# Block sums of the values: one batch stays on TensorE, the other goes to VectorE

## The chip, the cores and the metric

One core of one Trainium2 chip runs the whole program. The metric is the device time of one execution in microseconds; a kernel's time is the median over its runs. The profile is of one further execution, whose span is measured from its first to its last instruction.

## What is computed

An attention layer over 2 batches, 8 heads, 768 positions and 64 dimensions a head, followed by two feed-forward layers. Each query sees the keys at a distance below 16, and one summary for each block of 32 keys (24 blocks). A summary's key is the maximum of the block's keys, its value the mean of the block's values. Only that mean is touched here:

```
v_sum = v.reshape(B, H, nb, block, D).mean(axis=3)
scores_s = scale * einsum('bhsd,bhnd->bhsn', q, k_sum) + log(block)
a = softmax(concatenate([scores_l_masked, scores_s], -1))
attn = a @ concatenate([v, v_sum], axis=2)
x = (attn_x @ w_a) * (attn_x @ w_b) @ w_out
h = x @ w_in;  out = maximum(0.01 * h, h) @ w_out2
```

## The kernel before

The 1,536 tokens are three chunks of 512. Attention is cut into 12 pairs, four to a chunk; a pair is two groups of 256 queries of two heads each. For a pair the kernel transposes the queries (`q_prep`, L508), multiplies them with the keys window by window (`scores`, L526), takes the row minimum of the negated scores with the mask added on VectorE (L539) and the exponential on ScalarE (L543), divides by the sum (`normal`, L551 to L553, VectorE), transposes the result (`p_transpose`, L561, copied out by L563) and multiplies with the values (`pv`, L573, written out by L583 and L584). Block maxima of keys are taken in `k_prep` (L480 to L497). In what follows "(6,0)" is the first group of pair 6; pairs 6 and later hold batch 1. At most two scores tiles (`pm`) and two transposed ones (`pt`) are alive.

`load_vb` brings a batch's values as six tiles of 128 half blocks, 16 rows of 64 dimensions each. `v_sums` (twice for a batch) multiplies them with the matrix `place`, which adds neighbouring half blocks and divides by 32, and a VectorE reduction (L453) adds the eight row slots left in the bank. `v_place` (L463) moves the rows of the eight heads to partitions 0 to 23, L470 copies them out, and GpSimd (L189) spreads them into the value windows that `pv` multiplies. Both batches use the same six tiles; afterwards these buffers become `x` tiles.

The feed-forward weights arrive as fp64 and are made fp32 pairs on the chip by `convert`, seven steps a piece: `low` (L338 VectorE, L342 ScalarE), `clamp` (L346), `shift` (L351), `join` (L357), `add` (L363), `high` (L368, ScalarE), `rest_of` (L371). The steps wait in a list, `bg`. `tick(n)` takes n of them from its head; `weights(key)` takes as many as it needs until the piece that is to be multiplied is done. Every step is tied behind the latest L539 issued so far:

```
with tc.issue_after(pace["after"].ins) ...:
    bg.pop(0)()
```

The first pieces are, in order, a0, b0, a1, b1, a2, b2, a3, b3, o0 to o3. Products of the first chunk with a0 to b1 run inside attention; a2, b2, a3, b3 follow as `first_product` (L591, 12 matmuls each), and after each half of such a product `interleave` runs a share of the remaining attention operations of pairs 4 to 7 (they are sorted by an order number) and then `tick(4)`. There are eight such places before the output products of the first chunk (with o0 to o3). The program is written in this order; the scheduler then lets each engine take, at any moment, the earliest written instruction whose inputs it believes ready.

Of the kernel before, what the change touches and what calls it, by code (L numbers as in the profile page):

```python
# [11 lines left out]
F32 = mybir.dt.float32  # L12
# [4 lines left out]
ALU = mybir.AluOpType  # L17
AX = mybir.AxisListType
# [3 lines left out]
def kernel(  # L22
# [12 lines left out]
    nc = tc.nc  # L35
    B, H, S, D = q.shape
    P = 128
    BLK = 32
    WIN = 16
    NB = S // BLK  # L40
# [41 lines left out]
    sm_p = att.enter_context(tc.tile_pool(name="sm", bufs=4))  # L82
# [9 lines left out]
    def at_bank():  # L92
        cnt["at"] += 1
        return bank(at_banks[cnt["at"] % len(at_banks)])
# [26 lines left out]
    NV = 2 * H * NB // P  # L121
    vb_tiles = [xp.tile([P, BLK // 2, D], F32, tag="x", name=f"vb{j}") for j in range(NV)]
    vs_t = {}
    bg = []

    pace = {"micro": 0.0, "bg": 3, "after": None}
    q_t, k_t, vb_t, vw_of = {}, {}, {}, {}
# [68 lines left out]
    LOAD, SIDE, PRODUCT = range(3)  # L196
# [3 lines left out]
    def attention_ops():  # L200

        ops = []
        seen = set()
        for i, p in enumerate(sum(pairs, [])):

            def add(at, kind, f, *args):
                ops.append((PER * i + at, kind, lambda: f(*args), i))

            for m, (b, hp) in enumerate(dict.fromkeys(x[:2] for x in p)):
                if (b, hp) not in seen:  # L210
                    seen.add((b, hp))
                    add(-18, LOAD, load_k, b, hp)
                    for j in range(2):
                        add(2 * m + j + -12, PRODUCT, k_prep, b, hp, j)
                    if hp == 0:
                        add(-5, LOAD, load_vb, b)
                        for j in range(2):
                            add(1 + j, PRODUCT, v_sums, b, j)
                        add(7, PRODUCT, v_place, b)
            add(-14, LOAD, load_q, i, p)  # L220
            add(-6, PRODUCT, q_prep, i, p)
            for j in range(2):
                add(4 * j, PRODUCT, scores, i, p, j)
                add(4 * j + 3, SIDE, normal, i, j)
                add(4 * j + 8, PRODUCT, p_transpose, i, j)
            add(1, LOAD, load_vw, i, p)
            add(9, SIDE, put_sums, i, p)
            add(PV, PRODUCT, pv, i, p)
        ops.sort(key=lambda o: o[:2])
        return ops  # L230
# [19 lines left out]
    for c in range(2):  # L250
        for o, c0, c1 in ((0, 0, W), (W, SC, P)):
# [3 lines left out]
                out=loc, in_=loc, compare_op=ALU.is_ge, fill=BIG,  # L255
# [3 lines left out]
                out=loc, in_=loc, compare_op=ALU.is_ge, fill=BIG,  # L259
# [10 lines left out]
    V0 = 32  # L270
    place = const.tile([P, P], F32, tag="place", name="place")
    nc.gpsimd.memset(place, 1.0 / BLK)
    for base, pattern, mult in ((2 * V0, [[-2, P]], 1), (1 - 2 * V0, [[2, P]], -1)):

        nc.gpsimd.affine_select(
            out=place, in_=place, compare_op=ALU.is_ge, fill=0.0,
# [150 lines left out]
    def v_sums(b, j):  # L427
# [26 lines left out]
            out=vb_t[b][:, j], in_=ps.rearrange("p (j d) -> p d j", d=D), op=ALU.add, axis=AX.X  # L454
        )

    def v_place(b):

        v0 = vb_t.pop(b)
        ps = at_bank()  # L460
        for h in range(H):
            j, r = divmod(h, HQ)
            nc.tensor.matmul(  # L463
                out=ps[0:NB, h * D : (h + 1) * D],
                lhsT=ident[:, r * V0 : r * V0 + NB],
                rhs=v0[:, j],
                start=True, stop=True,
            )
        vs = sm_p.tile([NB, H, D], F32, tag="vs", name="vs", bufs=2)
        nc.scalar.copy(out=vs, in_=ps[0:NB].rearrange("p (h d) -> p h d", h=H))  # L470
        vs_t[b] = vs
# [165 lines left out]
    n_first = len(pairs[0])  # L637
    end = PER * (n_first - 1) + PV
    ops = attention_ops()
    for kt in range(NP):  # L640
        ops.append((PER * kt + PV + 5, PRODUCT, lambda kt=kt: early(kt), 0))
# [30 lines left out]
    def first_product(key, src, c):  # L672

        w = weights(key)
        ps = product_bank(key[0])
        for kt in range(KT):
            kt_mm(ps, w, src[c, kt], kt)
            if kt == KT // 2 - 1:
                interleave()
        return ps  # L680
# [114 lines left out]
    for f, c in slices2:  # L795
        ps = first_product(("i", f), ysp, c)
        h = g_p.tile([P, T], F32, tag="g", name="h")
        nc.scalar.copy(out=h, in_=ps)  # L798
        nc.vector.scalar_tensor_tensor(  # L799
            out=h, in0=h, scalar=0.01, in1=ps, op0=ALU.mult, op1=ALU.max  # L800
# [41 lines left out]
```

## Time and profile before

| | |
|---|---|
| time, median of 3 runs | 662.0 us (661.85 to 664.17) |
| the profiled execution | 662.39 us, of which the span is 660.7 us |
| PE (TensorE matmul) busy | 643.6 us, 97% of the span |
| DVE (VectorE) busy | 413.1 us, 63% |
| ACT (ScalarE) busy | 268.6 us, 41% |
| POOL (GpSimd) busy | 21.2 us, 3% |

The shares are means over the whole span; attention, on which the change works, ends for the first two chunks within the first 120 us, and is read in stretches of its own. A matmul of fp32 numbers appears as two records in this kernel's attention part.

### The profile page before, as it was taken

The numbers are of one execution on the slowest core, as the hardware profiler recorded it, in microseconds if no ns is written. First come the engines' busy times: TensorE is split into PE (matmuls) and PEld (weight loads), VectorE is DVE, ScalarE is ACT, GpSimd is POOL, SyncE is SP. The second block draws the span as 40 slices with busy tenths as digits, with TensorE's granted clock in tenths as the row PEclk, the third lists the DMA queues.
The fourth block names the chain that finished last, engine by engine and source line by source line (L and its number), as shares of the span: only waits on it lengthen the run. The fifth ranks groups of instructions, "written<-read, shape, count | busy, mean of one in ns | idle before, by whom it ended". The sixth has DMA issues, their size and how long they took to land.

```text
span 660.7 us, 9453 instructions
## 1 busy us (share of the span) xinstructions
PE 643.6 (97%) x3520; PEld 520.1 (79%) x3520; DVE 413.1 (63%) x960; ACT 268.6 (41%) x607; POOL 21.2 (3%) x39
## 2 busy tenths in 40 slices
PE   6798999999999999999999999999999999999997
PEld 4576767777888888888888888888888888888886
DVE  4978889955999972699633869732279532422323
ACT  4667767653445421344221535322255322222221
POOL 3111011000000000000000000000000000000000
PEclk9999999999999999999999999999999999999999
DMA  9977526411344430233200132400014000100101
GB/s 235 245 180 182 136 71 162 134 26 64 108 143 132 154 101 0 64 126 112 82 0 1 63 97 70 154 1 0 1 46 146 0 1 0 65 1 0 64 0 65
DMA packets 72591, 53.45 MB, mean 81 GB/s; under 512 B 46176, under 2 KB 66656, under 8 KB 72544
## 3 DMA queue, kind: packets, MB, share of 16 engines
q1 hardware_dynamic: 72544, 52.84, 27.7%
q8 instruction: 28, 0.46, 0.3%
q14 instruction: 19, 0.16, 0.1%
HBM read 49.68 MB, written 3.15 MB: 80 GB/s over the span
## 4 chain that ended last, share of the span: by engine, by line
PE 91%; DVE 4%; SPq 2%; DMA 1%; ACT 1%; issue 1%; ACTq 0%
PE ps_t L591 38%; PE ps_c L591 19%; PE ps_a L591 14%; PE ps_b L591 14%; PE ps_t L526 3%; PE ps_t L573 2%; PE ps_t L561 2%; PE ps_t L445 1%; SPq L175 1%; DMA wst<-in_moe_w_a_dram 1%; DMA wst<-in_moe_w_b_dram 1%; PE ps_t L508 1%; DVE pm L553 1%; SPq L132 0%; DVE pm L539 0%
## 5 line engine op out<-in xcount | busy, mean ns | idle before, releaser
L591 PE MATMUL ps_t<-x,wsp 128*128 128x512 f32 x336 | 78.6, 389 | 0.0
L591 PE MATMUL ps_c<-wsp,gs 128*128 128x512 f32 x288 | 75.8, 389 | 0.0
L591 PE MATMUL ps_t<-wsp,gs 128*128 128x512 f32 x288 | 74.7, 389 | 0.0
L591 PEld LDWEIGHTS ps_t<-x,wsp 128*128 128x128 f32 x336 | 63.1, 188 | 13.1
L591 PE MATMUL ps_t<-ys,wsp 128*128 128x512 f32 x288 | 71.9, 389 | 0.0
L591 PE MATMUL ps_a<-x,wsp 128*128 128x512 f32 x252 | 66.3, 399 | 1.4 <-DVE x L584 1.0
L342 ACT ACTIVATE wc<-wst 128x512 f32<-128x512 f32 x68 | 45.7, 675 | 53.7 <-DMA wst<-in_moe_w_out_dram 16.4
L591 PE MATMUL ps_b<-x,wsp 128*128 128x512 f32 x252 | 65.9, 395 | 0.0
L591 PEld LDWEIGHTS ps_t<-ys,wsp 128*128 128x128 f32 x288 | 54.1, 188 | 11.2
L591 PEld LDWEIGHTS ps_c<-wsp,gs 128*128 128x128 f32 x288 | 54.0, 188 | 11.2
L591 PEld LDWEIGHTS ps_t<-wsp,gs 128*128 128x128 f32 x288 | 54.0, 188 | 11.2
L591 PE MATMUL ps_c<-gs,wsp 128*128 128x512 f32 x240 | 60.3, 391 | 0.0
L591 PEld LDWEIGHTS ps_a<-x,wsp 128*128 128x128 f32 x252 | 46.4, 188 | 12.0 <-DVE x L584 1.5
L591 PEld LDWEIGHTS ps_b<-x,wsp 128*128 128x128 f32 x252 | 46.9, 188 | 9.8 <-issue 0.3
L799 DVE SCALAR_TENSOR_TENSOR h<-h,ps_t 128x512 f32<-128x512 f32 x24 | 16.5, 688 | 60.8 <-ACT h L798 60.8
L371 DVE TENSOR_TENSOR wsp<-wc,wsp 128x512 fp32r<-128x512 f32 x68 | 47.4, 700 | 9.1 <-ACT wsp L368 8.9
L591 PEld LDWEIGHTS ps_c<-gs,wsp 128*128 128x128 f32 x240 | 44.7, 188 | 9.3
L368 ACT CAST wsp<-wc 128x512 fp32r<-128x512 f32 x68 | 42.1, 622 | 20.5 <-DVE wc L363 13.9
L591 PE MATMUL ps_t<-gs,wsp 128*128 128x512 f32 x192 | 47.7, 390 | 0.0
L612 DVE TENSOR_TENSOR gs<-h,gs 128x512 fp32r<-128x512 f32 x48 | 33.1, 692 | 22.8 <-ACT gs L611 22.7
L363 DVE CUSTOM_DVE_ANT_0 wc<-wc,wr 128x1024 uint16<-128x1024 uint16 x68 | 46.9, 689 | 0.5
L357 DVE SCALAR_TENSOR_TENSOR wc<-wst,wc 128x512 int32<-128x512 int32 x68 | 46.5, 688 | 0.2
(89 smaller groups left out, 840.3 us busy)
## 6 DMA issues: line engine op xcount, KB each, us to landing
wst<-in_moe_w_out_dram SPq DMA_DIRECT2D x28, 512.0 KB, 3.3
wst<-in_moe_w_in_dram SPq DMA_DIRECT2D x16, 512.0 KB, 3.8
wst<-in_moe_w_a_dram SPq DMA_DIRECT2D x12, 512.0 KB, 3.8
wst<-in_moe_w_b_dram SPq DMA_DIRECT2D x12, 512.0 KB, 3.6
k<-in_k_dram SPq DMA_DIRECT2D x16, 192.0 KB, 4.5
vb<-in_v_dram SPq DMA_DIRECT2D x6, 512.0 KB, 5.2
out_dram<-acc SPq DMA_DIRECT2D x12, 256.0 KB, 2.1
q<-in_q_dram SPq DMA_DIRECT2D x16, 128.0 KB, 3.5
```

Of the source, the lines that this page charges most:

```text
L175: nc.sync.dma_start(out=t[p0 : p0 + o1 - o0, c, w0:w1, :], in_=src)
L342: nc.scalar.activation(out=t["c"].bitcast(F32), in_=hi_w.bitcast(F32), func=AF.Abs)
L357: nc.vector.scalar_tensor_tensor(out=t["c"], in0=hi_w, scalar=-0x40000000, in1=t["c"], op0=ALU.bitwise_and, op1=ALU.bitwise_or,)
L363: nc.vector.tensor_tensor(out=t["c"], in0=t["c"], in1=t["r"], op=ALU.add)
L368: nc.scalar.copy(out=t["w"][:, 0], in_=t["c"].bitcast(F32))
L371: nc.vector.tensor_tensor(out=t["w"][:, 1], in0=t["c"].bitcast(F32), in1=t["w"][:, 0].bitcast(F32), op=ALU.subtract,)
L526: nc.tensor.matmul(out=ps[h, w, :], lhsT=qt[h, w * W : (w + 1) * W], rhs=kts[h, (g * G + w) * SC : (g * G + w) * SC + P], start=True, stop ...
L561: nc.tensor.transpose(ps[:, w, :], pm[:, w, :], ident)
L573: nc.tensor.matmul(out=ps[c * D : (c + 1) * D, j * GT + w * W : j * GT + (w + 1) * W], lhsT=vw[:, c, j * G + w, :], rhs=pt[:, w, c * W : ( ...
L591: nc.tensor.matmul(out=ps, lhsT=w(a), rhs=x(b), start=first and j == 0, stop=last and j == 2)
L612: nc.vector.tensor_tensor(out=t[:, 1], in0=src, in1=t[:, 0].bitcast(F32), op=ALU.subtract)
L799: nc.vector.scalar_tensor_tensor(out=h, in0=h, scalar=0.01, in1=ps, op0=ALU.mult, op1=ALU.max)
```

## The change

For batch 0 nothing is changed. For batch 1 the two calls of `v_sums` go. In their place, earlier in the order (order number 44 in place of 49 and 50), `v_sums_later` puts twelve VectorE reductions at the head of `bg`: two for each of the six tiles, each adding the 16 rows of a half block for 32 of the 64 dimensions, straight from SBUF. They are taken by `tick`, four at a place, ahead of what is left of the conversions. `v_place` first takes whatever of the twelve is still in the list; for batch 1 it multiplies the tiles of half block sums with `place`, which now adds the halves, divides and moves in one: ten matmuls (five for each four heads) where there were eight.

```diff
+                        if b == 0:
+                            for j in range(2):
+                                add(1 + j, PRODUCT, v_sums, b, j)
+                        else:
+                            add(-4, SIDE, v_sums_later, b)
...
+    def v_sums_later(b):
+        vb_t[b] = v0 = sm_p.tile([P, NV, D], F32, tag="v1", name="v1", bufs=1)
+        bg[0:0] = [
+            lambda i=i, d=d: nc.vector.tensor_reduce(
+                out=v0[:, i, d : d + D // 2],
+                in_=vb_tiles[i][:, :, d : d + D // 2].rearrange("p j d -> p d j"),
+                op=ALU.add, axis=AX.X,
+            )
+            for i in range(NV)
+            for d in (0, D // 2)
+        ]
+        vb_done.append(bg[2 * NV - 1])
...
     def v_place(b):
+        while vb_done and vb_done[-1] in bg:
+            bg.pop(0)()
         v0 = vb_t.pop(b)
         ps = at_bank()
-        for h in range(H):
+        for h in range(H) if b else ():
+            r0, r1 = 2 * h * NB, 2 * (h + 1) * NB
+            tiles = range(r0 // P, (r1 - 1) // P + 1)
+            for i in tiles:
+                c0 = V0 + (r0 - i * P) // 2
+                nc.tensor.matmul(
+                    out=ps[0:NB, h * D : (h + 1) * D],
+                    lhsT=place[:, c0 : c0 + NB],
+                    rhs=v0[:, i],
+                    start=i == tiles[0], stop=i == tiles[-1],
+                )
+        for h in range(H) if not b else ():
```

## Rows read from the trace of the kernel before

**Rows 1.** The page, busy time of each engine, and PE's busy tenths in 40 slices.
```profile
PE 643.6 (97%) x3520; PEld 520.1 (79%) x3520; DVE 413.1 (63%) x960; ACT 268.6 (41%) x607; POOL 21.2 (3%) x39
PE   6798999999999999999999999999999999999997
```

**Rows 2.** Busy time by stretch; columns: stretch, length, engines, granted clock, DMA share, GB/s.
```profile
60.00:64.00 4.00, 2.93 (x14) 2.15 (x13) 4.00 (x9) 3.17 (x12) 0.00 (x0) 1.00 0.78 206
...
73.00:81.00 8.00, 8.00 (x70) 6.19 (x65) 7.36 (x19) 6.01 (x22) 0.00 (x0) 1.00 0.41 116
81.00:87.20 6.20, 6.20 (x49) 1.90 (x46) 2.63 (x12) 2.13 (x9) 0.00 (x0) 1.00 0.08 19
87.20:92.00 4.80, 4.80 (x75) 4.06 (x76) 4.76 (x17) 3.63 (x12) 0.00 (x0) 1.00 0.62 154
```

**Rows 3.** The chain that ended last, 77 to 92 us; columns: start, us, what.
```profile
77.14 0.46 PE ps_a L591 x2
...
77.82 2.32 PE ps_a L591 x10
80.14 1.02 PE ps_t L526 x16
81.16 1.85 PE ps_t L445 x16
...
83.60 3.60 PE ps_t L445 x24
87.20 0.59 PE ps_t L508 x4
87.78 0.44 PE ps_t L561 x4
...
89.24 0.56 PE ps_t L463 x8
89.80 1.08 PE ps_t L573 x32
...
91.44 0.66 PE ps_b L591 x2
```

**Rows 4.** The timeline of DVE, 72 to 92 us; idle before in brackets.
```profile
72.95 0.69 DVE L363 CUSTOM_DVE_ANT_0 wc<-wc,wr 128x1024 uint16<-128x1024 uint16 x1
73.55 0.68 DVE L553 TENSOR_TENSOR pm<-pm,sm 128x512 f32<-128x512 f32 x1
...
74.75 0.42 DVE L338 TENSOR_SCALAR wr<-wst 128x512 int32<-128x512 uint32 x1
...
75.35 0.69 DVE L371 TENSOR_TENSOR wsp<-wc,wsp 128x512 fp32r<-128x512 f32 x1
...
77.18 0.69 DVE L623 TENSOR_TENSOR g<-ps_b,g 128x512 f32<-128x512 f32 x1 [0.24 <-PE ps_b L591]
...
80.46 0.31 DVE L497 COPY kts<-ks 128x288 f32<-128x288 f32 x1
83.64 0.29 DVE L539 CUSTOM_DVE_ANT_0 pm<-ps_t,negm_first 128x128 f32<-128x128 f32 x1 [2.87 <-PE ps_t L561]
...
85.47 0.69 DVE L453 TENSOR_REDUCE v<-ps_t 128x64 f32<-128x512 f32 x1 [0.56 <-PE ps_t L445]
86.08 0.42 DVE L346 TENSOR_SCALAR wc<-wc 128x512 f32<-128x512 f32 x1
...
90.74 0.42 DVE L338 TENSOR_SCALAR wr<-wst 128x512 int32<-128x512 uint32 x1
91.08 0.68 DVE L371 TENSOR_TENSOR wsp<-wc,wsp 128x512 fp32r<-128x512 f32 x1
```

**Rows 5.** PE by stretch, earlier in attention; columns: stretch, length, PE, granted clock, DMA.
```profile
30.00:32.00 2.00, 1.17 (x7) 0.87 1.18 312
32.00:34.00 2.00, 2.00 (x11) 0.50 1.13 216
34.00:36.00 2.00, 2.00 (x31) 0.78 0.89 262
```

More of the change, by code (lines that the diff above doesn't have):

```diff
@@ L123 @@
     vs_t = {}
-    bg = []
+    bg, vb_done = [], []
     pace = {"micro": 0.0, "bg": 3, "after": None}
@@ L216, in attention_ops @@
                         add(-5, LOAD, load_vb, b)
-                        for j in range(2):
-                            add(1 + j, PRODUCT, v_sums, b, j)
+                        if b == 0:
[3 more added lines that the diff above has]
+                            add(-4, SIDE, v_sums_later, b)
                         add(7, PRODUCT, v_place, b)
```

## The prediction, made before the changed kernel was built or run

> **What bounds the kernel now.** I read the page first: TensorE is busy for 643.6 of 660.7 us, and after the first five of the 40 slices it never falls below nine tenths [rows 1]. VectorE's 63% is a mean that hides what matters here, so I went to the stretches. From 60 to 64 us PE is busy for only 2.93 of 4 us while DVE has no idle moment; from 64 us on PE is full, and from 73 to 81 us DVE works 7.36 of 8 us beside it [rows 2]. So the last part of attention is close to balanced: PE sets the time, DVE runs at its heels. Between 81 and 87.2 us the picture turns, PE full, DVE busy for 2.63 us only [rows 2]. That is batch 1's `v_sums`: on the chain of waits its matmuls (L445) hold 1.85 and 3.60 us [rows 3], and on DVE's timeline the pause shows as 2.87 us ahead of L539, which waits for a transpose (L561) that PE issued between the two calls [rows 4]. The last thing to see is how late the weights are made. Counting L371, the seventh ends a3 at 75.35 us and the eighth b3 at 91.08 [rows 4]; PE begins with a3 at 77.14 and with b3 at 91.44 [rows 3]. The conversions are made just before they are used, on the engine that now gets more to do.
>
> **What goes.** Both calls of `v_sums` of batch 1: 1.85 + 3.60 = 5.45 us of PE [rows 3]. The 40 records take far less than the sum of their durations because four column groups run beside each other, so I take their place on the chain and not their durations. PE has no pause around them, so all of it is on the path. On DVE two L453 go, 0.61 us each (85.47 to 86.08) [rows 4], 1.22 us together.
>
> **What comes on PE.** `v_place` of batch 1 has ten matmuls for eight. The eight are 16 records, two groups like that at 89.24 us with 0.56 us for 8 records [rows 3], 0.07 us a record. Two matmuls are four records, 0.28 us. If PE never waited, the change would be worth 5.45 - 0.28 = 5.17 us. The six loads of values are the same ones, and their tiles come free after the reductions as before after the matmuls: nothing is priced there.
>
> **What comes on DVE.** Twelve reductions of 512 numbers a partition. No reduction from SBUF stands in the trace; L453, also over 512 strided numbers but from PSUM, takes 0.61 us. The cheapest DVE row of that size from SBUF is L338, 0.34 us (90.74 to 91.08) [rows 4]; the dearest reading is the full 0.69 us of L453 with nothing overlapped. I take 0.61, the row that is the same operation: 7.32 us, between 4.1 and 8.3. The Trainium skill (VectorE: DVE Perf Modes, The perf-mode tier table) gives tensor_reduce a single rate wherever its data lies, while single-source operations on SBUF run at up to twice that; by it the low end falls away, and the sum stays at 7.32 us. L453 bears it out for PSUM; for SBUF no row here does. The Trainium skill's rules for kernel authors on the same page go further and advise to restructure such reductions on a hot path, which is the opposite of this change; what that would do here is the forecast below.
>
> **Where the twelve land.** They are taken four at a time at the second, third and fourth of the eight places in the first chunk's products. The first eight are tied behind (5,1)'s L539, which ends at about 72.95 us, the last four behind (6,1)'s. The list's tail moves with them: a3's `add`, `high` and `rest_of`, which before came in the second place, are now taken after the twelve, by `weights` ahead of a3's product, so behind (6,1)'s L539; b3 follows behind (7,0)'s and (7,1)'s. So DVE does not merely get 7.3 us more, it gets them ahead of a3.
>
> DVE until a3: before, its work from 72.95 us ends at 80.77 (80.46 + 0.31) with one pause of 0.24 [rows 4]. I take out that pause, a3's L363 (0.60) and L371 (0.60, the spacing of its size) and b3's L338 (0.34), and put in eight reductions (4.88): 80.77 - 0.24 - 1.54 + 4.88 = 83.87 us. The four L539 of a group take 0.85 us: from 83.64 to 84.91 (85.47 less its pause of 0.56) lie four of them and one L346 of 0.42 [rows 4]. With (6,0) and (6,1) it is 85.57; four reductions, 2.44, make 88.01; (6,0)'s L553 0.60 and a3's L363 0.60, 89.21; the cast on ScalarE, put at 0.60 by the same size, 89.81. Only then can PE begin with a3.
>
> PE until a3: without a3's first two matmuls it is free at 77.82 - 0.46 = 77.36 us [rows 3]. What it can do until then is attention: three score groups (6,0), (6,1), (7,0), 3 x 1.02; three transposes at 0.44, 1.32; two query transposes at 0.59, 1.18; `pv` of pair 5, 1.08; `v_place`, 1.12 + 0.28 [rows 3]. That is 8.04 us in a stretch of 12.45 us. **The cover is gone: PE idles for about 4.4 us**, because a3's product, which filled this stretch before, now lies behind it. No other filler exists: b3 comes later still, the output products need o0, and the second chunk's products need pairs 6 and 7. After 89.8 us a3 and b3, each 2.78 us (0.46 + 2.32), cover the rest of pairs 6 and 7, and once pair 7 is through, PE has the second chunk's products with weights that are ready. I count no further idle time.
>
> What is late next: the pieces o0 to o3 move back by twelve steps too. They are wanted by the first chunk's output products, and PE can put second-chunk products before those. I price this at nothing; without that cover it costs up to the steps of one piece, three of 0.34 and three of 0.60 us, 2.8 us.
>
> **The sum.** 662.39 us of the profiled execution - 5.17 + 4.4 = 661.6. The median of the three runs is 0.4 us below the profiled one, so I forecast 661.2 us, for a measurement that tells about 0.5%, 3.3 us, from no change. With reductions at 0.34 us a3 is ready 12 x 0.27 = 3.2 us sooner, the idle time is 1.2 us, and the time 658.0; with 0.69 us it is 12 x 0.08 = 1.0 us more, 662.2.
>
> **Rivals.** *Nothing is lost.* The scheduler, which believes a3 ready earlier or the reductions shorter, orders a3's three steps before most of the reductions, and these fill the 2.87 us pause and its two small followers. PE then stays full: 662.0 - 5.17 = 656.8 us, and up to 1.9 us of idle time would still be faster. For it speaks that DVE was idle for 3.57 of the 6.2 us that go [rows 2]; against it, the tie behind (6,1)'s L539 and the 12 reductions, which are twice that.
>
> *PE's order is wrong.* It ends slower. PE takes instructions as they were ordered when the program was made. If a3's product stands ahead of (7,0)'s scores, (5)'s `pv` and `v_place`, these 1.02 + 0.59 + 1.08 + 1.40 = 4.1 us wait with it, the softmax behind them starves DVE, and b3, all of whose 2.8 us of steps follow, is late in the same way: 4.4 + 4.1 + 2.8 = 11.3 us idle, 662.0 - 5.17 + 11.3 = 668.1 us. From 8.5 us of idle time on (5.17 + 3.3) the kernel is slower. Against it: before, PE was given b3 at the very moment it was made, with other work placed ahead.
>
> *The clock falls.* After its longest pauses in early attention PE's granted clock went from 1.00 to 0.50, 1.2 in place of 2.4 GHz; the three stretches at 0.87, 0.50 and 0.78 [rows 5] cost 2 x (0.13 + 0.50 + 0.22) = 1.7 us. If the new idle time lies in one piece, the same follows: 661.2 + 1.7 = 662.9 us. The Trainium skill (TensorE: Matmul & The Clock Gate, HAM oscillation) states the rule, that waits between bursts of matmuls throttle the array again and each burst then starts cold; [rows 5] agree. Against it: between 60 and 64 us PE idled for over a quarter of the time and the clock stayed at 1.00 [rows 2].
>
> **Chances.** Forecast 0.42, nothing lost 0.30, wrong order 0.18, clock 0.10. The first and last lie within 0.5% but for 0.02 on the slow side: faster 0.30, same 0.50, slower 0.20. The range reaches toward 656.8 below, and halfway to 668.1 above: 657.0 to 666.0. The forecast's own range, from the reductions' price and the late pieces, is 658.0 to 665.0.
>
> **What the profile after would show.** No matmuls of `v_sums` after 20 us, and 20 records in place of 16 in batch 1's `v_place`; twelve DVE reductions of 128x32 from 128x512 at about 0.6 us, eight of them between 73 and 84 us, four around 86 to 88; a3's L371 near 90 us; PE pauses between 77 and 90 us that add up to 4 us, full again afterwards. Wrong if a3 is ready before 80 us, if a reduction takes 0.4 us or less, if PE pauses again after 92 us, or if the order around a3 leaves PE waiting with attention work behind it.

## The result, and the profile after

The changed kernel is slower by 0.56%: median 666.46 us (7 runs, 665.35 to 668.62) against 663.36 us of the kernel before (7 runs beside it, 661.85 to 664.28), a ratio of 1.0056 with an interval of 1.0034 to 1.0079. The forecast was 661.2 us, no change; the time lies 0.5 us above the wider of its two ranges (657.0 to 666.0). The profiled execution after took 668.49 us, the longer end of its runs, so its span is compared with some care. In the changed kernel's line numbers what was L363, L371, L445, L463, L539 and L591 is L366, L374, L448, L494, L570 and L622, and the scores' L526 is L557 (lines up to `v_sums` move by 3, those behind it by 31); the cast `high`, L368 before, is L371 now. The new reductions are L464, `v_place`'s new matmuls for batch 1 L486.

The page after (span, busy time, PE's tenths), against [rows 1]:

```profile
span 666.8 us, 9394 instructions
...
PE 643.2 (96%) x3484; PEld 520.7 (78%) x3484; DVE 417.7 (63%) x964; ACT 269.1 (40%) x607; POOL 19.7 (3%) x39
...
PE   6799798999999999999999999999999999999997
```

PE has 36 instructions fewer: 40 of `v_sums` gone, four of `v_place` added, as forecast. Yet its busy time fell by 0.4 us only, and the fifth and the seventh slice are no longer full. VectorE has 4.6 us more work and 4 instructions more. Six reductions came and two L453 went, so there are **six reductions, not the twelve of the prediction**, from three tiles of a batch and not six (`NV` = 2 x 8 x 24 / 128 = 3). The busy time by stretch, with the columns of [rows 2]:

```profile
73.00:81.00 8.00, 5.67 (x58) 4.02 (x57) 7.09 (x17) 5.33 (x23) 0.00 (x0) 1.00 0.54 139
81.00:87.00 6.00, 4.42 (x28) 3.38 (x28) 6.00 (x15) 2.37 (x6) 0.00 (x0) 0.72 0.14 31
87.00:92.00 5.00, 4.28 (x70) 3.73 (x72) 3.02 (x20) 4.09 (x17) 1.77 (x3) 1.00 0.25 57
100.00:110.00 10.00, 7.67 (x38) 5.40 (x39) 6.47 (x22) 5.34 (x19) 0.27 (x1) 1.00 0.87 186
```

Before, PE had no pause in the first three [rows 2]. Now it lacks 2.33, 1.58 and 0.72 us, 4.63 together, and again 2.33 between 100 and 110, where it was full before too (10.00 of 10.00); between 92 and 100 and after 110 us it is full in both. In the second row the granted clock is 0.72. VectorE's side of this, its timeline, against [rows 4]:

```profile
75.50 5.74 DVE L464 TENSOR_REDUCE v<-vb 128x32 f32<-128x512 f32 x6
81.16 0.68 DVE L366 CUSTOM_DVE_ANT_0 wc<-wc,wr 128x1024 uint16<-128x1024 uint16 x1
81.76 0.69 DVE L584 TENSOR_TENSOR pm<-pm,sm 128x512 f32<-128x512 f32 x1
82.36 0.69 DVE L521 TENSOR_REDUCE ks<-ps_t 128x16 f32<-128x512 f32 x1
...
91.01 1.05 DVE L374 TENSOR_TENSOR wsp<-wc,wsp 128x512 fp32r<-128x512 f32 x1
```

The six stand in one block, 5.66 us from 75.50 to 81.16, 0.94 us apart. Behind them begins a3's `add` (L366), which before ran at 72.95; its `rest_of` (L374), 75.35 before, begins at 91.01 [rows 4]. The timeline of PE, with the idle time ahead and what ended it in brackets:

```profile
77.72 0.95 PE L622 MATMUL ps_b<-x,wsp 128*128 128x512 f32 x3
82.55 1.22 PE L622 MATMUL ps_a<-x,wsp 128*128 128x512 f32 x2 [3.88 <-ACT wsp L371]
83.56 0.63 PE L511 MATMUL ps_t<-ident,k 128*128 128x128 f32 x2
84.12 1.82 PE L557 MATMUL ps_t<-kts,qt 64*64 64x128 f32 x16
...
87.22 1.30 PE L486 MATMUL ps_t<-v,place 128*24 128x64 f32 x20 [0.25 <-ACT qt L543]
...
91.24 1.09 PE L557 MATMUL ps_t<-kts,qt 64*64 64x128 f32 x16 [0.50 <-DVE nb L570]
92.26 0.69 PE L604 MATMUL ps_t<-pt,vw 128*64 128x64 f32 x16
92.88 2.58 PE L622 MATMUL ps_a<-x,wsp 128*128 128x512 f32 x10
...
101.61 2.56 PE L622 MATMUL ps_b<-x,wsp 128*128 128x512 f32 x10 [0.67 <-DVE wsp L374]
...
106.91 0.50 PE L622 MATMUL ps_a<-x,wsp 128*128 128x512 f32 x1 [1.61 <-ACT x L614]
```

In PE's order a3's first two matmuls stand ahead of the key transposes (L511) and the scores (L557). They need only a3's high half (`high`, L371 on ScalarE, after L366), and it comes at 82.5: 3.88 us of pause in one piece. The other ten, which need the rest, were placed much later and wait for nothing at 92.88. The scores right after the pause take 1.82 us for 16 records where they otherwise take 1.09. PE's granted clock there, columns stretch, length, PE, clock, DMA share, GB/s:

```profile
82.00:84.00 2.00, 1.45 (x4) 0.56 0.29 66
84.00:86.00 2.00, 2.00 (x18) 0.58 0.07 16
86.00:88.00 2.00, 1.75 (x22) 1.00 0.14 32
```

Near 1.2 GHz in place of 2.4 for two of these stretches: 2 x (0.44 + 0.42) = 1.7 us, an estimate at the high end, since PE stood idle for the first 0.55 us of them. The second pause has two parts. Ahead of b3's product PE waits 0.67 us for its `rest_of` (L374, 101.61 above); the other 1.61 us end with a cast on ScalarE (L614). How that came, from the chain that ended last:

```profile
99.39 6.47 DMA wst<-in_moe_w_out_dram
```

The timeline of SP (SyncE), which asks for loads:

```profile
90.41 7.83 SPq L175 DMA_DIRECT2D vw<-in_v_dram  x12
98.34 0.93 SPq L141 DMA_DIRECT2D q<-in_q_dram  x2
99.39 0.44 SPq L316 DMA_DIRECT2D wst<-in_moe_w_out_dram  x1
```

And the timeline of ScalarE:

```profile
105.94 0.66 ACT L345 ACTIVATE wc<-wst 128x512 f32<-128x512 f32 x1 [4.05 <-DMA wst<-in_moe_w_out_dram]
106.50 0.36 ACT L614 CAST x<-ps_t 128x256 fp32r<-128x256 f32 x1
```

The raw weights of o1 (`w_out`) are asked for at 99.39 us only; before it was 88.86. b3's `join` (L360), the last to read the buffer that they go into, ran at 96.78 in place of 87.92, and on SP twelve loads of value windows (L175) and two of q stand ahead of them. They land 6.47 us later. ScalarE stood 4.05 us at L345 for them, and the cast of x (L614) behind it in its order, which PE wanted, waited too.

**The account** from the profile, by its own terms: -5.17 (the forecast's saving) + 4.63 (pauses 73 to 92) + 1.7 (clock) + 2.33 (pauses 100 to 110) = +3.5 us. The medians differ by 3.1. The two profiled spans differ by 6.1, of which 1.3 lies before anything the change touches (the first product of x begins at 61.79 against 60.52, with one order on all engines up to there); the 1.3 left over are no pauses. Most of them are PE's own busy time: from 120 to 200 us the same 64 score records (L557, L526 before) keep PE busy for 5.22 us in place of 4.36, 0.9 us more. In the order after, other matmuls cut two of their groups, into 12 and 4 records (0.87 + 0.43 us) and into 4, 2 and 10 (0.43 + 0.43 + 0.86), where a whole group of 16 takes 1.09. Both these differences are smaller than what the runs of one kernel scatter (2.4 us before, 3.3 after).

### The profile page after: what moved, and what is told of

Its sections match the earlier page's. It is cut to its first block, busy times and chain, and to the rows that moved or that the text cites. A ratio compares the mean times of both kernels' runs of the same rounds, so it can differ in the third digit from the quotient of the medians.

```text
span 666.8 us, 9394 instructions
## 1 busy us (share of the span) xinstructions
PE 643.2 (96%) x3484; PEld 520.7 (78%) x3484; DVE 417.7 (63%) x964; ACT 269.1 (40%) x607; POOL 19.7 (3%) x39
## 3 DMA queue, kind: packets, MB, share of 16 engines
HBM read 49.68 MB, written 3.15 MB: 79 GB/s over the span
## 4 chain that ended last, share of the span: by engine, by line
PE 88%; DMA 4%; DVE 3%; ACT 2%; SPq 1%; issue 1%; ACTq 0%
PE ps_t L622 37%; PE ps_c L622 18%; PE ps_a L622 13%; PE ps_b L622 13%; PE ps_t L557 3%; PE ps_t L592 1%; ACT pm L574 1%; DMA k<-in_k_dram 1%; PE ps_t L604 1%; DMA wst<-in_moe_w_out_dram 1%; DMA wst<-in_moe_w_b_dram 1%; DMA wst<-in_moe_w_a_dram 1%; DVE v L464 1%; DMA vw<-in_v_dram 1%; SPq L175 0%
## 5 line engine op out<-in xcount | busy, mean ns | idle before, releaser
L622 PE MATMUL ps_t<-x,wsp 128*128 128x512 f32 x336 | 78.4, 389 | 0.0
L622 PE MATMUL ps_c<-wsp,gs 128*128 128x512 f32 x288 | 75.8, 389 | 0.0
L622 PE MATMUL ps_t<-wsp,gs 128*128 128x512 f32 x288 | 74.7, 389 | 0.0
L622 PE MATMUL ps_a<-x,wsp 128*128 128x512 f32 x252 | 66.6, 402 | 7.2 <-ACT wsp L371 3.9
L622 PEld LDWEIGHTS ps_t<-x,wsp 128*128 128x128 f32 x336 | 63.1, 188 | 13.1
L622 PE MATMUL ps_t<-ys,wsp 128*128 128x512 f32 x288 | 71.9, 389 | 0.0
L345 ACT ACTIVATE wc<-wst 128x512 f32<-128x512 f32 x68 | 45.9, 676 | 58.1 <-DVE wsp L374 15.9
L622 PE MATMUL ps_b<-x,wsp 128*128 128x512 f32 x252 | 64.7, 394 | 0.7 <-DVE wsp L374 0.7
L622 PEld LDWEIGHTS ps_c<-wsp,gs 128*128 128x128 f32 x288 | 54.1, 188 | 11.2
L622 PEld LDWEIGHTS ps_t<-ys,wsp 128*128 128x128 f32 x288 | 54.1, 188 | 11.2
L622 PEld LDWEIGHTS ps_t<-wsp,gs 128*128 128x128 f32 x288 | 54.0, 188 | 11.2
L622 PEld LDWEIGHTS ps_a<-x,wsp 128*128 128x128 f32 x252 | 46.5, 189 | 18.2 <-ACT wsp L371 4.3
L622 PE MATMUL ps_c<-gs,wsp 128*128 128x512 f32 x240 | 60.7, 393 | 0.0
L622 PEld LDWEIGHTS ps_b<-x,wsp 128*128 128x128 f32 x252 | 46.8, 188 | 10.5 <-DVE wsp L374 1.1
L371 ACT CAST wsp<-wc 128x512 fp32r<-128x512 f32 x68 | 42.2, 622 | 27.6 <-DVE wc L366 21.1
L374 DVE TENSOR_TENSOR wsp<-wc,wsp 128x512 fp32r<-128x512 f32 x68 | 46.8, 689 | 9.6 <-ACT wsp L371 9.4
L622 PEld LDWEIGHTS ps_c<-gs,wsp 128*128 128x128 f32 x240 | 44.4, 188 | 9.5 <-ACT x L614 0.2
L366 DVE CUSTOM_DVE_ANT_0 wc<-wc,wr 128x1024 uint16<-128x1024 uint16 x68 | 47.5, 699 | 0.3
L622 PE MATMUL ps_t<-gs,wsp 128*128 128x512 f32 x192 | 47.5, 390 | 0.0
L360 DVE SCALAR_TENSOR_TENSOR wc<-wst,wc 128x512 int32<-128x512 int32 x68 | 46.3, 684 | 0.3
```

The costliest lines, as they stand in the source:

```text
L345: nc.scalar.activation(out=t["c"].bitcast(F32), in_=hi_w.bitcast(F32), func=AF.Abs)
L360: nc.vector.scalar_tensor_tensor(out=t["c"], in0=hi_w, scalar=-0x40000000, in1=t["c"], op0=ALU.bitwise_and, op1=ALU.bitwise_or,)
L366: nc.vector.tensor_tensor(out=t["c"], in0=t["c"], in1=t["r"], op=ALU.add)
L371: nc.scalar.copy(out=t["w"][:, 0], in_=t["c"].bitcast(F32))
L374: nc.vector.tensor_tensor(out=t["w"][:, 1], in0=t["c"].bitcast(F32), in1=t["w"][:, 0].bitcast(F32), op=ALU.subtract,)
L622: nc.tensor.matmul(out=ps, lhsT=w(a), rhs=x(b), start=first and j == 0, stop=last and j == 2)
```

## The experiments

All ratios are to the kernel before, run beside them (medians 663.2 to 663.4 us). The main theories set against each other: that the time added on VectorE decides, in a stretch where it has none to spare; and that the block's place decides, ahead of a3's weights. Runs that leave out or change a part of the sums say so in their expectation.

### The same reductions over neighbouring numbers (e1_contiguous)

```diff
-                in_=vb_tiles[i][:, :, d : d + D // 2].rearrange("p j d -> p d j"),
+                in_=vb_tiles[i].rearrange("p j d -> p (j d)")[:, 16 * d : 16 * d + 512]
+                    .rearrange("p (d j) -> p d j", j=16),
```

> The six reductions read the same tile in runs of 16 neighbouring numbers in place of one number every 256 bytes; their count, shapes and place are those of the changed kernel (which sums then go into which block is no longer that of the reference). Theory A, the reductions' length ahead of a3 makes PE wait: if the stride makes them long (0.94 us each), they fall to about 0.61 us, six are 2.0 us shorter, the 3.9 us pause shrinks to about 1.9 us, and the time comes down by 2 us or more, toward 1.000 to 1.003 of before. Theory B, the new order on PE loses the time whatever the reductions take: the ratio stays near 1.0056. If the stride is not the reason, each stays at 0.94 us and nothing moves.

663.56 us, ratio 1.0001 [0.9987, 1.0015]. The rows of the reductions by source line, with duration minimum, median and maximum, first of the changed kernel:

```profile
L464 DVE TENSOR_REDUCE v<-vb x6: 999/1030/1058, 75.5 to 80.2; 128x32 f32<-128x512 f32 x6
```

and of this one:

```profile
L464 DVE TENSOR_REDUCE v<-vb x6: 674/676/682, 74.3 to 77.3; 128x32 f32<-128x512 f32 x6
```

The shape is the same, so 0.35 us of each reduction is the step of 64 numbers (256 bytes) with which it reads SBUF. Starts are (77.3 - 74.3)/5 = 0.60 us apart in place of 0.94. PE's order is that of the changed kernel, and its timeline shows what is left of the pause:

```profile
79.29 0.73 PE L622 MATMUL ps_a<-x,wsp 128*128 128x512 f32 x2 [0.75 <-ACT wsp L371]
```

0.75 us in place of 3.88, and the clock stays at 1.00. The pauses from 73 to 92 add up to 1.78 us, from 92 to 110 to 0.71. By these the kernel should still be 2.7 us faster than before; it is level. In the profiled pair 1.4 us come ahead of the first product of x (61.9 against 60.5), and from 120 us on the scores are cut as in the changed kernel (5.22 us of PE in place of 4.36); why the medians are level isn't shown beyond that. What is shown: up to 115 us PE, VectorE and ScalarE run the order of the changed kernel, so the 2.9 us between the two are the length of the six reductions and what followed from it.

### Two of sixteen rows read (e2_short)

```diff
-                in_=vb_tiles[i][:, :, d : d + D // 2].rearrange("p j d -> p d j"),
+                in_=vb_tiles[i][:, 0:2, d : d + D // 2].rearrange("p j d -> p d j"),
```

> Each reduction adds only 2 of the 16 rows (64 numbers in place of 512), so the work of the block sums is left out but for an eighth. Same place ahead of a3. Theory A: the six take about 1 us together, the pause before a3 is gone or below 0.5 us, PE's clock stays at 1.00, and the time falls below before, 0.991 to 0.996. Theory B: PE's order is almost that of the changed kernel, so it stays above 1.002.

658.86 us, ratio 0.9925 [0.9908, 0.9942]. Six reductions of 0.22 us make 0.8 us; no pause ahead of a3, and 0.97 us in small ones from 73 to 92. The whole of the saving on PE was there to be had: 5.17 - 1.1 = 4.1 us by the pauses, 4.5 measured. Over the three kernels with six reductions in the same place on VectorE, their block takes 0.8, 3.6 and 5.66 us and the median is 658.86, 663.56 and 666.46: 7.6 us of time for 4.9 us of VectorE, 1.6 for one. Only the last two have one order on PE (2.9 us for 2.1, 1.4 for one); in this kernel it differs from 81.8 us on, where a transpose cuts `v_place`, so a part of its 4.7 us may be the order.

### a3's weights finished ahead of the reductions (e3_a3_first)

```diff
+    def half_sum(v0, i, d):
+        with tc.issue_after(made["a", 3].ins):
+            nc.vector.tensor_reduce(...)
...
-        bg[0:0] = [
+        bg.extend([
```

`made` holds each conversion's `rest_of`, the instruction behind which the scheduler may place the reductions; they also go to the end of the list in place of its head.

> The six reductions at full length, but tied behind a3's last conversion step. Theory A (place): a3 is ready near 76 us as before, its product covers the reductions, the 3.9 us pause goes, ratio 0.992 to 0.998. Theory C (amount: VectorE has 5.7 us more to do at a place where it is already full, wherever they stand): the pause only moves to the next product or softmax, ratio 1.000 to 1.006.

665.17 us, ratio 1.0029 [1.0014, 1.0043]: place alone gives back 1.3 of 3.1 us, and the interval still overlaps the changed kernel's. Its timeline of PE:

```profile
77.14 2.54 PE L626 MATMUL ps_a<-x,wsp 128*128 128x512 f32 x10
82.04 1.97 PE L561 MATMUL ps_t<-kts,qt 64*64 64x128 f32 x16 [2.36 <-DVE ks L525]
```

and of VectorE:

```profile
75.77 0.69 DVE L374 TENSOR_TENSOR wsp<-wc,wsp 128x512 fp32r<-128x512 f32 x1
76.38 3.96 DVE L462 TENSOR_REDUCE v<-vb 128x32 f32<-128x512 f32 x4
...
80.35 0.97 DVE L462 TENSOR_REDUCE v<-vb 128x32 f32<-128x512 f32 x1
...
81.58 0.41 DVE L525 TENSOR_REDUCE ks<-ps_t 128x8 f32<-128x256 f32 x1
```

a3's product runs at 77, as before [rows 3]. Five reductions now hold up the key sums (L525) in its stead; the scores wait for them, 2.36 us, and the clock is 0.72 from 81 to 87 us here too. The wait went from one consumer of VectorE to the next. PE's pauses from 73 to 110 us are 5.1 us; with 1.7 for the clock and less 5.17 that makes 1.6 us lost, 1.8 measured.

### The reductions added, nothing taken away (e4_both)

```diff
                         for j in range(2):
                             add(1 + j, PRODUCT, v_sums, b, j)
+                        if b:
+                            add(-4, SIDE, v_sums_extra, b)
```

> The kernel before, which still sums batch 1 on TensorE, with the six reductions added at the same place and their results unused. Theory A: a3 is late by about the reductions' time, and with the TensorE sums as cover PE loses some of it: 1.003 to 1.009 of before. Theory B: the order on PE keeps its cover, so below 1.002.

670.39 us, ratio 1.0098 [1.0071, 1.0125]: 7.0 us lost. PE pauses for 1.53 us from 73 to 92 and 0.52 from 92 to 110, at full clock. The two `v_sums` calls of batch 1 hold PE for 3.56 us each until its next work starts, 7.1 in place of 5.45 [rows 3]. These make 3.7 us. The profiled execution is the fastest of the four (668.60), 6.2 us longer than the profiled one of before; what pauses and `v_sums` leave of these is PE's busy time again: the 384 score records keep it busy for 30.51 us in place of 28.43 over the whole span, since other matmuls cut their groups (at 87.92 us into 10, 2 and 4 records, 0.87 + 0.43 + 0.43 us). So the reductions cost time in this kernel too, in part by pauses and in part by an order in which PE takes longer for the same matmuls.

### The sums on GpSimd (e5_gpsimd)

```diff
+        for n in (8, 4, 2):
+            for t in vb_tiles:
+                nc.gpsimd.tensor_tensor(out=t[:, 0:n], in0=t[:, 0:n], in1=t[:, n : 2 * n], op=ALU.add)
+        for i, t in enumerate(vb_tiles):
+            nc.gpsimd.tensor_tensor(out=v0[:, i], in0=t[:, 0], in1=t[:, 1], op=ALU.add)
```

> The half block sums move from VectorE to GpSimd, as additions of halves of the tile (16 rows to 8, 4, 2, 1), not tied to anything; TensorE keeps the new v_place. Nothing of the reference is left out. Theory C, what counts is the VectorE time added where VectorE is full: with none added, the change keeps its 5.2 us and the ratio is 0.991 to 0.995, like the short reductions. Rival D: GpSimd's additions are slow or slow VectorE down beside them, so v_place or VectorE's steps come late: 0.998 or more.

661.32 us, ratio 0.9972 [0.9962, 0.9982]. From 73 to 87 us PE is full. But the additions were placed early; the timeline of POOL:

```profile
30.66 1.38 POOL L189 COPY vw<-vs 24x1024 f32<-24x1024 f32 x1
32.12 4.75 POOL L465 TENSOR_TENSOR vb<-vb 128x512 f32<-128x512 f32 x4
44.75 1.03 POOL L189 COPY vw<-vs 24x1024 f32<-24x1024 f32 x1 [7.88 <-PE ps_t L601]
```

They run between GpSimd's spreading of block sums (L189), which attention waits for (the row of four joins two additions of 512 numbers and two of 256), and PE is busy for 11.63 of the 20 us from 20 to 40 where it was 15.76. VectorE was slowed beside them too: `normal`'s multiplication (L553 before) took 1.61 us at 32.31 us in place of 0.68. Of the 5.17 us the kernel keeps 2.0, between the two expectations; the 4.1 lost here are more than the 3.2 that it doesn't keep, so a part is caught up later.

### The sums by halving additions on VectorE (e6_tree)

```diff
+        def half(n, i):
+            t = vb_tiles[i]
+            out = t[:, 0:n] if n > 1 else v0[:, i : i + 1]
+            nc.vector.tensor_tensor(out=out, in0=t[:, 0:n], in1=t[:, n : 2 * n], op=ALU.add)
+        bg[0:0] = [lambda n=n, i=i: half(n, i) for n in (8, 4, 2, 1) for i in range(NV)]
```

> The sums stay on VectorE at the same place, but as twelve additions of contiguous halves (three each of 512, 256, 128 and 64 numbers). By rows of the kernel before (0.60 us for 512, about 0.33 for 256) they take about 3 x (0.60 + 0.33 + 0.20 + 0.13) = 3.8 us in place of 5.7, close to the six contiguous reductions (3.6 us, ratio 1.0001). Theory C: 0.998 to 1.003. If only the number of instructions ahead of a3 mattered, twelve would be worse than six: above 1.006.

660.15 us, ratio 0.9961 [0.9948, 0.9974], faster than before with the same mathematics. Its rows by line and shape, busy time and mean of one:

```profile
L466 DVE TENSOR_TENSOR vb<-vb 128x512 f32<-128x512 f32 x3 | 1.9, 683 | 0.0
L466 DVE TENSOR_TENSOR vb<-vb 128x256 f32<-128x256 f32 x3 | 1.2, 414 | 0.0
L466 DVE TENSOR_TENSOR vb<-vb 128x128 f32<-128x128 f32 x3 | 0.8, 273 | 0.0
L466 DVE TENSOR_TENSOR v<-vb 128x64 f32<-128x64 f32 x3 | 0.6, 217 | 0.0
```

4.5 us of busy time, against 3.6 in e1_contiguous and 5.7 in the changed kernel, and yet faster than e1_contiguous: the amount is not all. The twelve stand in small groups from 72.9 to 85.6 us among the key sums and the softmax, and the scheduler placed a3's twelve matmuls on PE behind `v_place`:

```profile
85.46 1.30 PE L483 MATMUL ps_t<-v,place 128*24 128x64 f32 x20
86.69 0.66 PE L589 MATMUL ps_t<-ident,pm 128*128 128x128 f32 x4
87.10 3.01 PE L619 MATMUL ps_a<-x,wsp 128*128 128x512 f32 x12
```

PE's pauses from 73 to 92 are 1.97 us, all under 0.8 us, and none follows until 110. 5.17 - 1.97 = 3.2 us; measured 3.15. Which of the two, grain or order, brings it, this run doesn't separate.

### A third buffer for raw weights (e7_third_buffer, e11_before_third_buffer)

```diff
-    wst_p = ctx.enter_context(tc.tile_pool(name="wst", bufs=2))
+    wst_p = ctx.enter_context(tc.tile_pool(name="wst", bufs=3))
```

In the changed kernel:

> The changed kernel with a third buffer for raw weights, so that o1's load need not wait until b3's join has read its buffer. Theory E, the second pause (2.3 us between 100 and 110 us, ScalarE waiting 4.05 us for that load): it goes, and the time falls by about 2 us, ratio 1.001 to 1.004. Rival: ScalarE's wait was covered, or the next wait takes its place: 1.005 and above.

662.84 us, ratio 0.9998 [0.9983, 1.0013], 3.6 us better than the changed kernel. Between 100 and 110 us PE is full (10.00), and ScalarE does not wait for o1's load any more, which is asked for at 74.57 in place of 99.39 us:

```profile
74.57 0.44 SPq L316 DMA_DIRECT2D wst<-in_moe_w_out_dram  x1
```

But the whole order from about 26 us on changed with it, and so did the first pause:

```profile
80.07 0.44 PE L511 MATMUL ps_t<-ident,k 128*128 128x128 f32 x2 [2.73 <-DVE ks L521]
80.26 0.71 PE L622 MATMUL ps_a<-x,wsp 128*128 128x512 f32 x2
```

One pause of 2.73 us, behind the key sums, and no fall of the clock. The pauses from 73 to 110 are 3.57 us in place of 6.96, and the clock's 1.7 are saved too; of these 5.1 us the median shows 3.6. b3's product still waits 0.53 us for its `rest_of`, at 97.38. The second pause alone wasn't isolated.

The control, the same buffer in the kernel before:

> The kernel before with a third buffer for raw weights, the control for the changed kernel's version with it (0.9998, that is 0.0058 below the changed kernel's 1.0056). Theory E, the buffer mends a wait that the change brought: 0.998 to 1.001 here, since PE has no pause after 64 us. Rival: the buffer is worth about 0.5% to any of these kernels: 0.993 to 0.996.

663.64 us, ratio 1.0011 [1.0001, 1.0021]: worth nothing without the change.

### The reductions forty microseconds earlier (e8_early)

```diff
-                        add(-5, LOAD, load_vb, b)
+                        add(-20 if b else -5, LOAD, load_vb, b)
...
-                            add(-4, SIDE, v_sums_later, b)
+                            add(-19, SIDE, v_sums_later, b)
```

The reductions are issued at once and not through the list `bg`.

> The same six reductions at full length, untied, and the load of their tiles, some 40 us earlier in the order, where VectorE has a pause of 2.75 us (33 to 36 us). Theory C: half of the 5.7 us hides in that pause, the rest delays VectorE there, while the part from 73 us on is as in the kernel with short reductions: ratio 0.994 to 1.000. Rival: the load is not there yet (it lands near 31 us), VectorE waits for it in order and all of early attention is late: 1.003 and above.

663.87 us, ratio 1.0007 [0.9994, 1.002]. They run from 29.6 to 37.2 us, and from 73 to 87 PE is full. From 20 to 40 us VectorE now works 19.73 of 20 us, and PE 13.81 where it was 15.76, at a granted clock of 0.76 in place of 0.91; from 60 to 73 us the clock is 0.87 in place of 1.00. The stretch of before with time to spare on VectorE is not the early one either.

### GpSimd behind its own spreading, alone and with the third buffer (e9, e10)

```diff
+        with tc.issue_after(spread["last"].ins):
             for n in (8, 4, 2):
```

`spread["last"]` is the last L189 issued when the sums are asked for.

> As the GpSimd version, but its twelve additions tied behind GpSimd's spreading of pair 4, so that they no longer stand ahead of the spreading for pairs 3 and 4. Theory C with D only early: the 10 us of GpSimd fall into its idle stretch from about 55 to 66 us, early attention is as before (PE busy about 15.7 of 20 us between 20 and 40 us, against 11.6 with the untied additions), and the whole 5.2 us are kept: ratio 0.990 to 0.994. If GpSimd's additions slow VectorE wherever they run: 0.997 or more.

661.13 us, ratio 0.9979 [0.9967, 0.999]. The additions run from 47.8 to 61.8 us, PE's 16.15 us from 20 to 40 are whole again, yet the time is that of e5_gpsimd, as the rival said. From 40 to 60 us PE is busy for 16.39 us where it was 17.98, and its waits for x from VectorE between 40 and 112 us are 3.4 us where they were 1.0. VectorE's timeline, with nine of the additions on GpSimd from 47.81 to 57.20, shows a cause:

```profile
47.93 1.75 DVE L374 TENSOR_TENSOR wsp<-wc,wsp 128x512 fp32r<-128x512 f32 x1
49.60 1.77 DVE L582 TENSOR_TENSOR pm<-pm,sm 128x512 f32<-128x512 f32 x1
51.30 1.76 DVE L366 CUSTOM_DVE_ANT_0 wc<-wc,wr 128x1024 uint16<-128x1024 uint16 x1
52.98 0.68 DVE L613 TENSOR_TENSOR x<-ps_t,x 128x512 fp32r<-128x512 f32 x1
```

The first three read both inputs from SBUF and take 1.75 to 1.77 us where before they take 0.68 to 0.69 [rows 4]; the fourth, of the same size, has one input in PSUM and keeps its 0.68. So work moved to GpSimd still costs time on VectorE. Later come 1.81 us of pauses from 60 to 73 (1.07 before), 0.45 until 92 and 0.87 until 110.

> The same with a third buffer for raw weights. If late loads cost time in this version too, 0.988 to 0.992; if they are covered, the same as without the buffer.

659.1 us, ratio 0.9947 [0.9933, 0.9961]. That lies between the two expectations. From 73 to 92 us PE misses 0.05 us, but 1.30 between 92 and 100.

### Halving additions and the third buffer (e12_tree_third_buffer)

> The additions on VectorE (ratio 0.9961) with a third buffer. If late loads are what is left of its pauses (1.3 us at 73 to 81 us, 0.7 at 81 to 87 us): 0.992 to 0.995; if VectorE's load alone makes them: 0.995 to 0.998.

659.04 us, ratio 0.9944 [0.9931, 0.9957], with e10 the fastest that computes the reference: 0.6% below before, 1.1% below the changed kernel. Against its control, e11_before_third_buffer, it is 4.6 us; 5.17 less its pauses from 73 to 92 of 0.64 us are 4.5. The order differs from e6_tree's as well, so how much of the 1.1 us between them is late loads isn't shown.

## Why the prediction was wrong

The steps that failed are two terms left out of the sum: the pieces that are late after a3, priced at nothing, where the runs showed 2.33 us of pauses between 100 and 110 us; and the clock after the forecast's own pause, kept at full, where it fell and cost 1.7 us. The price and number of the reductions were wrong too, without much effect on the sum.

**What bounds, what goes, what comes on PE: right.** VectorE at PE's heels was the point (of PE's slices the last is a 7, which "never falls below nine tenths" passes over). The 36 records and 5.17 us stand: e2_short, e6_tree and e12_tree_third_buffer recover them less their own pauses, to 0.5 us. `v_place` has 20 records and 1.30 us where 1.40 were counted.

**What comes on VectorE: two errors that nearly cancel.** "Twelve reductions" failed: the 6 loads in the trace were taken for six tiles of one batch, but are three for each of two batches, and `NV` = 3 gives six reductions; the description of the kernel and of the change ahead of the prediction has the same error. "I take 0.61, the row that is the same operation" failed too: L453 reads PSUM, and from SBUF with that step it is 0.94. The sum is 5.66 us in place of 7.32. The low end (0.34) and the dear end (0.69) both missed; e1_contiguous shows 0.60 for the same operation from neighbouring numbers, so L453 was the right row for the operation and said nothing of the step. The Trainium skill (VectorE: DVE Perf Modes, The perf-mode tier table) has one rate for tensor_reduce; 0.60 against 0.94 differ from that, and the measurement decides. The Trainium skill (SBUF — State Buffer, Door 1: The DMA port swizzle) says that SBUF is read in 16-byte lines and that each step onto a new line costs; e1_contiguous agrees in the sign. Had this page been weighed, the price would have been a rival.

**Where they land: partly right.** Ahead of a3, yes; "four at a time", no: all six ran in one block behind (5,1)'s L570. And a3's `add` was not tied behind (6,1)'s: it ran at 81.16, ahead of (6,0)'s L570 at 87.25. a3's rest came near 90 as forecast (91.01), but its high half, for which PE's order already had two matmuls waiting ahead of keys and scores, at 82.5. The rival of PE's order is this mechanism, at a smaller price than its 4.1 + 2.8 us, since ten of the twelve matmuls were placed late.

**The pause from 73 to 92: 4.4 forecast, 4.63 measured**, though for other reasons: a longer price, fewer reductions, an earlier wait. That the two numbers agree is luck.

**"What is late next ... I price this at nothing" failed.** So did "I count no further idle time". The pieces after a3 were late, and a cover did not exist: 2.33 us from 100 to 110, within the 2.8 given as the price without cover. 0.67 of them are b3's own lateness, 1.61 the cast behind o1's load. With a third buffer (e7_third_buffer) ScalarE's wait for that load is gone and PE is full there. What I hadn't seen is the way there: conversions made later free the raw-weight buffers later (b3's `join` at 96.78 in place of 87.92), so a load starts later (99.39 in place of 88.86), and ScalarE stands at it with other work behind.

**The clock, a rival at 0.10, came true on top:** 1.7 us, the size named. It should have hung on the forecast's own 4.4 us pause: my forecast held that pause and gave full clock to what followed. The 1.00 of the stretch from 60 to 64 [rows 2] was no evidence against it: that idle time came in two pieces, of 0.41 and 0.66 us, each ahead of a product of x. The Trainium skill's rule (TensorE: Matmul & The Clock Gate, HAM oscillation) that the burst behind a wait starts cold agrees with the 0.56 and 0.58 here.

So the forecast's 661.2 us should have had 2.3 and 1.7 added: 665.2 us. These two terms, both named in the prediction and both left out of its sum, are 4.0 of the 5.3 us by which it missed. The rest is near the 1.4 us by which the median of the kernel before itself came out higher beside the changed one (663.36) than in the runs the forecast started from (662.0).

**The theories.** That place alone decides fell with e3_a3_first. VectorE's time decides between e1_contiguous and the changed kernel, where nothing else changes; e2_short fits it, with another order on PE from 81.8 us on. e6_tree shows that the grain or the order it leads to moves 3.4 us beside it. A third way of losing time, an order that cuts PE's score groups, is seen in the changed kernel, e1_contiguous and e4_both, but no run tests it alone. Open are the rest in e1_contiguous, some of which lies ahead of anything that the change touches, and why the scheduler placed a3's first two matmuls where it did.

## What to carry to other kernels

When an engine at 63% on average has no idle moment in the stretch where the work lands, each microsecond added there can cost more than one: here 1.4 to 1.6. Follow what it delays to the buffers that come free later and the loads behind them, and if the forecast itself holds a pause of several microseconds in PE, price the cold clock after it too (1.7 us here, nothing in e7_third_buffer). In this kernel sums over a strided axis of SBUF were better made by halving additions over whole rows, in small steps that other work passed between, than by strided reductions: 6.3 us.

## What the runs showed of the hardware

- A VectorE reduction of 512 fp32 numbers a partition from SBUF: 0.94 us apart with a step of 256 bytes, 0.60 with neighbouring numbers; from PSUM with a step of the same kind L453 took 0.61 [rows 4].
- GpSimd adds 128x512 fp32 numbers in 1.26 to 1.73 us (e5_gpsimd, e9_gpsimd_late); VectorE makes three such additions in a row in 1.89 us (e6_tree).
- Beside these additions VectorE's operations with two inputs in SBUF take up to 1.77 us in place of 0.69; one that reads PSUM keeps its 0.68 (e9_gpsimd_late).
- 16 score records take PE 1.09 us in one group and 1.72 us in pieces of 4, 2 and 10 among other matmuls (after).
- After a pause of 3.88 us (after) and of 2.36 us (e3_a3_first) the granted clock fell, to 0.56 and 0.58 for two stretches of 2 us in the first; after one of 2.73 us (e7_third_buffer) it stayed at 1.00. The length of the pause alone doesn't say it.
